# Seven half-size products for eight in the first layer of experts 1 to 3, with the tokens' combinations kept in DRAM

## The chip, the cores and the metric

The kernel runs on one core of a Trainium2 chip. The metric is device time in microseconds of that core. The core has a matrix engine (PE; its weight loads are listed apart as PEld), three engines for element-wise work (DVE, ACT, POOL), a queue that issues most DMA transfers (SP), an on-chip memory SBUF, eight PSUM banks of 2 KB per partition into which PE accumulates, and DRAM outside.

## The reference

Three stages run one after the other: a causal retention (linear attention with decay), a mixture of four experts in which every token passes through every expert, and a second mixture of eight experts in which each token goes to one. All inputs are float32. Only the second stage is changed. Cut to it:

```python
N, D, E, F = 2304, 512, 4, 1024
p = domain_probs / (domain_probs.sum(-1, keepdims=True) + 1e-09)
out = np.zeros((N, D))
for e in range(E):
    h = np.maximum(x @ w1[e], 0.0)          # the first layer: the part that is changed
    out += p[:, e:e + 1] * (h @ w2[e])
```

## The kernel before, in words

Every float32 operand of a matmul is split into two float16 numbers, a high and a low part, and a product is made of three float16 matmuls (high by high, high by low, low by high; `TERMS`). The split takes one ACT instruction (the high part) and one DVE instruction (the low part; `split`, lines 160 to 162).

The retention runs in 24 steps of 96 tokens (`at_load`, `at_split`, `at_a`, `at_b`). The output of a step is scaled by DVE (`xf`, line 269); ACT writes its high part and POOL its low part into the resident tile `xT` (lines 271 and 272), which holds all 2304 tokens. Steps 0 to 3 run ahead of everything; the other twenty are called between the matmuls of expert 0 (`at_hook`).

The second stage runs over four experts and, in each, over six blocks of 384 tokens; one expert with one block is called a pass here. A pass has eight units of the first layer (`l1`: 12 matmuls of 384 columns into one PSUM bank, then ACT writes relu's high part and DVE its low part into `ht`, lines 326 and 327) and three of the second (`l2`: 24 matmuls of 512 columns, then one ACT or DVE instruction into `acc`, lines 346 and 348). There are two banks (`ph`) for the first layer and two (`po`) for the second. The next expert's weights are loaded and split during the passes (`w_hook`: expert 1's in expert 0's last pass, the others' from the expert's third pass on). Through all passes of experts 1 to 3 the weights of the second mixture are loaded, split and stored back to DRAM (`s_hook`). In expert 3's passes, transposes and gate logits of the finished tokens (`g1`, `g2`, `g3`) stand between the other matmuls, in two PSUM banks of their own.

A scheduler lays the instructions out on each engine at build time, by the program's order and by what it takes to be ready. At run time each engine's queue is worked off in that order, and an instruction that waits on a semaphore holds up all that stand behind it on its engine. SP's queue of DMA issues works in the same way.

Of the kernel before, what the change touches and what calls it, by code (L numbers as in the profile page):

```python
# [9 lines left out]
F32 = mybir.dt.float32  # L10
# [11 lines left out]
C = 96  # L22
# [14 lines left out]
BIG = 65536.0  # L37
TERMS = ((0, 0), (0, 1), (1, 0))
# [63 lines left out]
def kernel(  # L102
# [48 lines left out]
    xT = x_p.tile([128, 2, KD, N], F16, name="xT")  # L151
# [4 lines left out]
    x1d = dram.tile([N, ROW], F32, name="x1d")  # L156
    w1d = dram.tile([E2 * 128, KD, 2, F], F16, name="w1d")
# [21 lines left out]
    raws, spl, pm, st = {}, {}, {}, {}  # L179

# [62 lines left out]
    def at_b(s):  # L243
# [52 lines left out]
    def w_split(e, i):  # L296
        r = rw.pop((e, i))
        if i < KD:
            w_parts(r, wt[e][0][:, i], None)
        else:  # L300
            j = 2 * (i - KD)
            w_parts(r, wt[e][1][:, j:j + 2], True)

# [4 lines left out]
    def l1(e, b, f, c0=0, c1=BT):  # L308
        w = wt[e][0]
        ph = ps.tile([128, BT], F32, tag="h", name="ph")  # L310
        t0 = b * BT
        n = 0
        for k in range(KD):
            for x, y in ((0, 0), (0, 1), (1, 0)):
                pe.matmul(  # L315
                    ph[:, c0:c1],
                    lhsT=w[:, k, x, f * 128:(f + 1) * 128],
                    rhs=xT[:, y, k, t0 + c0:t0 + c1],
# [4 lines left out]
        if c0 == 0:  # L323
            hts[f] = ht_p.tile([128, 2, BT], F16, tag="ht", name="ht")
        hi, lo, p = hts[f][:, 0, c0:c1], hts[f][:, 1, c0:c1], ph[:, c0:c1]
        pace["act"] = act.activation(out=hi, in_=p, func=ACTF.Relu)  # L326
        pace["dve"] = dve.scalar_tensor_tensor(out=lo, in0=p, scalar=0.0, in1=hi, op0=ALU.max, op1=ALU.subtract)  # L327

    def l2(e, b, i):
# [4 lines left out]
        for k in range(KF):  # L334
            for x, y in ((0, 0), (0, 1), (1, 0)):
                pe.matmul(  # L336
                    po,
                    lhsT=hts[k][:, x, i * 128:(i + 1) * 128],
# [15 lines left out]
    def s_load(i):  # L354
        e, j = divmod(i, 8)
        r = later["pool"].tile([128, 1024], F32, tag="sr", name="sr", bufs=2)
# [27 lines left out]

    def g1(t, pl):
        tp = later["ps"].tile([128, KD, 128], F32, tag="tp", name="tp")
# [6 lines left out]
    def g2(t):  # L393
        xs = x1h.pop(t)
        pg = later["ps"].tile([128, 2 * E2], F32, tag="pg", name="pg")
# [7 lines left out]
    def g3(b, pl):  # L403
# [13 lines left out]
        pr = later["ps"].tile([128, 2, TB * E2], F32, tag="pg", name="pr")  # L417
# [44 lines left out]
    def unpermute(pl, rr, tiles, n, name):  # L462

        pi = later["ps"].tile([128, n], F32, tag="pg", name="pi" + name)
# [152 lines left out]
    def m_open():  # L617
        x_ctx.close()
        p = ctx.enter_context(tc.tile_pool(name="m2", bufs=1, side="right"))
# [86 lines left out]
    def l1_part(c0, c1):  # L706
        for f in range(KF):
            l1(0, 0, f, c0 * C, c1 * C)
# [37 lines left out]
    wgr = const.tile([128, KD, 2 * E2], F32, name="wgr")  # L746
# [3 lines left out]
    ps_sum = const.tile([128, NT, 1], F32, name="ps_sum")  # L750
    dve.tensor_reduce(out=ps_sum, in_=p_sb, axis=AX.X, op=ALU.add)
    dve.tensor_scalar(out=ps_sum, in0=ps_sum, scalar1=1e-9, scalar2=None, op0=ALU.add)
    ps_inv = const.tile([128, NT, 1], F32, name="ps_inv")
# [10 lines left out]
    w_at = {}  # L764

    def at_hook():
# [191 lines left out]
```

## Time and profile before

| | |
|---|---|
| median of 3 runs | 1099.6 us (1098.09 to 1100.0) |
| the profiled execution, its own time | 1101.13 us |
| its span, first to last instruction | 1099.4 us |
| granted clock of PE, mean | 0.989 |
| busy: PE, DVE, ACT, POOL | 96%, 43%, 32%, 16% of the span |
| retention alone, before expert 0's second block | 0 to 92.46 us |
| expert 0's blocks 1 to 4, with retention between | 92.46 to 259.88 us |
| expert 0's block 5, then experts 1 and 2 | 259.88 to 680.30 us |
| expert 3 with the gate | 680.30 to 865.00 us |
| second mixture | 865.00 to 1099.4 us |

The span is the time between the first and the last instruction on the core; the profiled execution's own time is 1.7 us longer, and 1.5 us above the median. The busy share of an engine is an average over stages that differ; what counts for a change is the stage in which it works.

### The profile page before, as it was taken

What the parts mean: (1) busy time and instruction counts of PE and PEld (TensorE: products, weight loads), DVE (VectorE), ACT (ScalarE), POOL (GpSimd) and SP (SyncE); (2) the same over time, 40 slices, a digit from 0 to 9 for tenths busy, and PEclk for the clock granted to TensorE, in tenths of its full rate; (3) what the DMA queues carried; (4) which work ended last, traced back from release to release, by engine and by line L of the source; (5) the groups of instructions that cost most, each with busy time, mean ns of one, the idle gap of its engine ahead of it and who ended that gap; (6) DMA issues with size and microseconds to landing.
All of it is one profiled execution on the core that took longest, in us unless ns stands there. A gap on an engine that the chain in (4) does not pass through costs nothing.

```text
span 1099.4 us, 21060 instructions
## 1 busy us (share of the span) xinstructions
PE 1056.7 (96%) x9057; PEld 635.0 (58%) x9057; DVE 477.0 (43%) x935; ACT 352.1 (32%) x683; POOL 178.9 (16%) x160
## 2 busy tenths in 40 slices
PE   4789999999999999999999999999999999999996
PEld 3665555555555555555555555555555677777774
DVE  5966555654333455433344544544444511111111
ACT  5544444534322244321222432322221122222221
POOL 5655646620000000000000000000000021212121
PEclk9889999999999999999999999999999999999998
DMA  8552322102343566434446554344413262491692
GB/s 249 170 178 79 97 59 73 45 1 88 106 137 131 172 211 193 146 122 127 142 137 208 154 154 136 114 125 145 163 49 133 108 224 96 154 351 53 241 378 112
DMA packets 38514, 158.30 MB, mean 144 GB/s; under 512 B 4878, under 2 KB 5262, under 8 KB 36112
## 3 DMA queue, kind: packets, MB, share of 16 engines
q1 hardware_dynamic: 34896, 145.84, 40.4%
q0 software_dynamic: 3520, 11.06, 2.9%
q8 instruction: 73, 1.20, 0.5%
q14 instruction: 25, 0.20, 0.1%
HBM read 159.99 MB, written 43.55 MB: 185 GB/s over the span
## 4 chain that ended last, share of the span: by engine, by line
PE 68%; issue 11%; DMA 10%; POOL 5%; DVE 4%; ACT 1%; SPq 0%; POOLq 0%; DVEq 0%; ACTq 0%
PE po L336 32%; PE ph L315 31%; DMA out_dram<-y_s,sidxm 8%; DMA out_dram<-y_s,sidxe 2%; POOL vs L195 1%; PE xo L251 1%; PE sc L213 1%; POOL v L202 1%; POOL p L219 1%; DMA vkr<-in_vk_dram 1%; DVE w L162 1%; PE tp L388 1%; POOL sn L237 1%; DVE pf L217 1%; POOL xT L272 1%
## 5 line engine op out<-in xcount | busy, mean ns | idle before, releaser
L315 PE MATMUL ph<-xT,w 128*128 128x384 f16 (+1 forms) x2400 | 388.5, 321 | 9.5 <-DVE ht L327 5.4
L336 PE MATMUL po<-w,ht 128*128 128x512 f16 x1728 | 382.8, 380 | 0.1
L315 PEld LDWEIGHTS <-w 128*128 128x128 f16 x2400 | 231.5, 98 | 153.1 <-issue 11.2
L336 PEld LDWEIGHTS <-ht 128*128 128x128 f16 x1728 | 168.1, 98 | 197.9 <-issue 2.1
L326 ACT ACTIVATE ht<-ph 128x384 f16<-128x384 f32 (+1 forms) x200 | 95.2, 477 | 360.1 <-PE ph L315 359.9
L327 DVE SCALAR_TENSOR_TENSOR ht<-ph,ht 128x384 f16<-128x384 f32 (+1 forms) x200 | 107.2, 539 | 165.4 <-ACT ht L326 157.2
L348 DVE SCALAR_TENSOR_TENSOR acc<-po,p_sb,acc 128x512 f32<-128x512 f32 x54 | 40.5, 750 | 189.7 <-PE po L336 189.7
L664 PEld LDWEIGHTS <-lane 128*128 128x128 f16 x1920 | 109.0, 98 | 4.3 <-issue 0.2
L664 PE MATMUL p_h<-x_s,lane 128*128 128x128 f16 x1920 | 111.1, 219 | 0.0
L681 PE MATMUL p_y<-lane,h_s 128*128 128x512 f16 x480 | 107.2, 379 | 0.8 <-DVE h_s L674 0.8
L640 POOL DMA_INDIRECT x_g<-x1d,gidxe x3 | 3.2, 1060 | 593.0 <-PE ph L315 592.4
L674 DVE SCALAR_TENSOR_TENSOR h_s<-p_h,h_s 128x512 f16<-128x512 f32 x40 | 27.6, 691 | 158.3 <-ACT h_s L673 158.3
L162 DVE SCALAR_TENSOR_TENSOR s<-sr,s 128x512 f16<-128x512 f32 x128 | 82.7, 687 | 7.4 <-ACT s L161 7.4
L681 PEld LDWEIGHTS <-h_s 128*128 128x128 f16 x480 | 46.6, 98 | 52.6 <-DVE h_s L674 1.0
L161 ACT ACTIVATE s<-sr 128x512 f16<-128x512 f32 x128 | 73.0, 620 | 7.1 <-DMA w2d<-s 4.5
L673 ACT ACTIVATE h_s<-p_h 128x512 f16<-128x512 f32 x40 | 23.9, 597 | 78.5 <-PE p_h L664 78.5
L162 DVE SCALAR_TENSOR_TENSOR w<-wr,w 128x512 f16<-128x512 f32 x64 | 45.3, 745 | 0.5 <-ACT w L161 0.5
L683 ACT ACTIVATE y_s<-p_y,x_g 128x512 f32<-128x512 f32 x20 | 13.7, 687 | 92.5 <-PE p_y L681 78.8
L684 POOL DMA_INDIRECT out_dram<-y_s,sidxm x17 | 17.3, 1018 | 146.7 <-ACT y_s L683 138.1
L161 ACT ACTIVATE xs<-tp 128x512 f16<-128x512 f32 x18 | 10.7, 597 | 82.9 <-PE tp L388 82.9
L217 DVE TENSOR_TENSOR pf<-sc,ka 96x384 f32<-96x384 f32 x48 | 24.3, 546 | 28.9 <-PE sc L213 28.9
L195 POOL TENSOR_TENSOR vs<-vkr,ka 96x512 f32<-96x512 f32 x24 | 35.2, 1465 | 10.3 <-DMA ka<-in_ca_dram 7.3
(141 smaller groups left out, 655.7 us busy)
## 6 DMA issues: line engine op xcount, KB each, us to landing
lane<-w1d SPq DMA_DIRECT2D x20, 2048.0 KB, 9.3
lane<-w2d SPq DMA_DIRECT2D x20, 2048.0 KB, 9.2
wr<-in_w_dram SPq DMA_DIRECT2D x32, 512.0 KB, 6.3
sr<-in_w1s_dram SPq DMA_DIRECT2D x32, 512.0 KB, 4.3
w1d<-s SPq DMA_DIRECT2D x32, 512.0 KB, 5.2
sr<-in_w2s_dram SPq DMA_DIRECT2D x32, 512.0 KB, 4.3
w2d<-s SPq DMA_DIRECT2D x32, 512.0 KB, 5.3
qkr<-in_qk_dram SPq DMA_DIRECT2D x24, 384.0 KB, 4.3
```

The lines of the kernel that those rows point to most:

```text
L161: act.activation(out=hi, in_=raw, func=ACTF.Copy, scale=scale)
L162: dve.scalar_tensor_tensor(out=lo, in0=raw, scalar=scale, in1=hi, op0=ALU.mult, op1=ALU.subtract)
L195: pool.tensor_tensor(out=vs, in0=t[:, 0], in1=cst("vtab", H, 1)[:C].to_broadcast([C, H, D]), op=ALU.mult)
L217: dve.tensor_tensor(out=pf, in0=sc[r], in1=mask, op=ALU.mult)
L315: pe.matmul(ph[:, c0:c1], lhsT=w[:, k, x, f * 128:(f + 1) * 128], rhs=xT[:, y, k, t0 + c0:t0 + c1], start=(n == 0), stop=(n == 3 * KD - 1),)
L326: pace["act"] = act.activation(out=hi, in_=p, func=ACTF.Relu)
L327: pace["dve"] = dve.scalar_tensor_tensor(out=lo, in0=p, scalar=0.0, in1=hi, op0=ALU.max, op1=ALU.subtract)
L336: pe.matmul(po, lhsT=hts[k][:, x, i * 128:(i + 1) * 128], rhs=w[:, k, y], start=(n == 0), stop=(n == 3 * KF - 1),)
L348: dve.scalar_tensor_tensor(out=a, in0=po, scalar=p_sb[:, t, e:e + 1], in1=a, op0=ALU.mult, op1=ALU.add)
L664: pe.matmul(ph[:, j], lhsT=w[:, k, x, f * 128:(f + 1) * 128], rhs=xs[:, y, k], start=(n == 0), stop=(n == 3 * KD - 1),)
L674: dve.scalar_tensor_tensor(out=lo, in0=ph, scalar=0.0, in1=hi, op0=ALU.max, op1=ALU.subtract)
L681: pe.matmul(po, lhsT=h[:, a, k], rhs=w[:, k, b], start=(n == 0), stop=(n == 3 * KF - 1))
```

## The change

The four quarters of an expert's first weights (halves of the 512 inputs by halves of the 1024 hidden units) and the halves of a block's tokens and inputs are combined beforehand, so that a block's first layer takes seven products of half size in each dimension instead of eight (the Winograd form of Strassen's scheme). `PROD` names for each product the combination of weights (0 to 6) and of tokens (0 to 7). It applies to experts 1 to 3; expert 0 multiplies the plain halves as before.

- Tokens: step by step the retention writes its result into a tile `xc` of one block (two of them take turns) instead of `xT`. For every second pair of steps `at_mix` makes four combinations: four POOL instructions of 192 columns, one ACT instruction (high parts) and one DVE instruction (low parts) of 768. Each finished block is stored to DRAM (`xcd`). From expert 0's last pass on, `x_load` fetches the next block's combinations once a pass: 10,752 bytes per partition, 1344 KB in two transfers. There are 18 such loads.
- Weights: `w_mixed` makes 14 quarter splits of 512 columns (7 combinations for each of 2 row blocks) where `w_split` made 8, with 8 POOL additions or subtractions of 512 columns between them, in place, in the raw tiles. The second layer's weights are split as before (8 of 512 columns). This is done in 24 steps of one call each; in expert 0's last pass three are called per unit; the calls for experts 2 and 3 begin in the second pass of the expert before, one every third unit.
- First layer: `l1_mixed` has 14 units of 12 matmuls of 192 columns (seven products, each for two pairs of hidden blocks `j`). PSUM banks carry sums on from product to product: ACT copies bank x into bank y, bank q into SBUF (s5) and x into a new bank z; DVE adds s5 to x twice. `keep` makes relu's two parts eight times per pass, of 384 columns each, as before. Per pass this adds six ACT copies and four DVE additions.
- PSUM: the new banks y and q (two each) take the four banks that were left, so the gate of expert 3 shares the two `po` banks until `m_open`. The raw tiles of both mixtures' weights share one pool of four buffers.

The core of the diff (left out: renamed tiles, unchanged parts of the loops):

```diff
+PROD = {1: (0, 0), 2: (1, 1), 4: (2, 7), 5: (3, 4), 6: (4, 5), 7: (5, 6), 3: (6, 3)}
...
+    def at_mix(s):
+        xa, xb = xfs.pop(s - 2), xfs.pop(s)
+        b, r = divmod(s, 4)
+        m = at_1.tile([128, 4, 2, C], F32, name="xm", bufs=1)
+        pool.tensor_tensor(out=m[:, 0], in0=xb[:, 0], in1=xa[:, 0], op=ALU.subtract)
...
+        act.activation(out=hi, in_=m, func=ACTF.Copy)
+        dve.tensor_tensor(out=lo, in0=m, in1=hi, op=ALU.subtract)
+        if r == 3:
+            sp.dma_start(out=xcd[b * 128:(b + 1) * 128], in_=xcs[b])
+    def x_load(b):
+        t = x_p.tile([128, 2, 8, 2, HB], F16, tag="xc", name="xc")
+        src = xcd[b * 128:(b + 1) * 128]
+        sp.dma_start(out=t[:, :, 0:2], in_=src[:, :, 0:2])
+        sp.dma_start(out=t[:, :, 3:], in_=src[:, :, 3:])
...
+        def rows(k, more):
+            steps.append(lambda: put(k, 3, 2))
+            steps.append(lambda: (mix(k, 3, 1, 3, ALU.add), put(k, 0, 0)))
+            steps.append(lambda: (mix(k, 1, 0, 1, ALU.subtract), put(k, 2, 1)))
+            steps.append(lambda: (mix(k, 0, 3, 0, ALU.subtract), put(k, 3, 3)))
+            steps.append(lambda: (mix(k, 2, 2, 0, ALU.subtract), put(k, 1, 5)))
+            steps.append(lambda: (put(k, 0, 4), more[0]()))
+            steps.append(lambda: (put(k, 2, 6), more[1]()))
...
+            for i in range(2):
+                f = (2 * j + i) * 128
+                n = 0
+                for k in range(2):
+                    for u, v in TERMS:
+                        pe.matmul(
+                            bank[:, i], lhsT=w[:, k, u, f:f + 128], rhs=x[:, v, d, k],
+                            start=(first and i == 0 and n == 0), stop=(n == 5), skip_group_check=True,
+                        )
...
+        def m7(j):
+            x_, s5 = t[j]["x"], t[j]["s"]
+            mm(x_, 7, j)
+            z = t[j]["z"] = bank("y", later["mix"])
+            cp = act.activation(out=z, in_=x_, func=ACTF.Copy)
+            ad = dve.tensor_tensor(out=s5, in0=x_, in1=s5, op=ALU.add)
...
+            keep(s5, out_to(1, j, 1))
...
+        for m in (m1, m5, m6, m2_, m7, m3, m4):
+            for j in range(2):
+                units.append(lambda m=m, j=j: m(j))
...
+    def g_bank(tag, shape, name=None):
+        if "ps" in later:
+            return later["ps"].tile(shape, F32, tag=tag, name=name or tag)
+        return ps.tile(shape, F32, tag="o", name=name or tag)
...
+                if u == 0 and e + (b == NB - 1) and (e, b) != (E1 - 1, NB - 1):
+                    x_load((b + 1) % NB)
```

POOL's queue at the end of retention step 7, the last of token block 1, before. `sn` is a state, `p`, `v` and `vs` belong to later steps, `xT` is step 7's low part:

```order
L237 TENSOR_TENSOR sn<-sn,ka 128x256 [waits DVE_49]
L219 TENSOR_TENSOR p_1435<-pf,p_1435 96x384 [waits Activation_49]
L202 TENSOR_TENSOR v_1559<-vs,v_1559 96x512 [waits Activation_49]
L195 TENSOR_TENSOR vs<-vkr,ka 96x512 [waits DMAHW6_49,Pool_49]
L272 TENSOR_TENSOR xT<-xf,xT 128x4x96 [waits Activation_49]
```
The same place now; `xm` are combinations of the step's tokens, `xc` is step 7's low part (the 128x4x96 row):

```order
L241 TENSOR_TENSOR sn<-sn,ka 128x256 [waits DVE_49]
L223 TENSOR_TENSOR p_1455<-pf,p_1455 96x384 [waits Activation_49]
L206 TENSOR_TENSOR v_1579<-vs,v_1579 96x512 [waits Activation_49]
L199 TENSOR_TENSOR vs<-vkr,ka 96x512 [waits DMAHW5_49,Pool_49]
L291 TENSOR_TENSOR xm<-xf 128x192 [waits DVE_49]
L292 TENSOR_TENSOR xm<-xf 128x192
L283 TENSOR_TENSOR xc<-xf,xc 128x4x96 [waits Activation_49]
```
Two combinations now stand between `vs` and the low part that the next pass's first matmuls read.

DVE's queue in expert 0's last pass before: `ht` is the low part of a first-layer unit, `w_1` are expert 1's weights:

```order
L162 SCALAR_TENSOR_TENSOR w_1_4337<-wr,w_1_4337 128x512 [waits Activation_49]
L327 SCALAR_TENSOR_TENSOR ht<-ph,ht 128x384 [waits Activation_49]
L162 SCALAR_TENSOR_TENSOR w_1_4337<-wr,w_1_4337 128x512 [waits Activation_49] x2
L327 SCALAR_TENSOR_TENSOR ht<-ph,ht 128x384 [waits Activation_49]
L162 SCALAR_TENSOR_TENSOR w_1_4337<-wr,w_1_4337 128x512 [waits Activation_49] x2
L327 SCALAR_TENSOR_TENSOR ht<-ph,ht 128x384 [waits Activation_49]
L162 SCALAR_TENSOR_TENSOR w_1_4337<-wr,w_1_4337 128x512 [waits Activation_49] x2
L327 SCALAR_TENSOR_TENSOR ht<-ph,ht 128x384 [waits Activation_49]
```
The same place now (4419 and 4421 are the two tiles of expert 1's first weights):

```order
L389 SCALAR_TENSOR_TENSOR ht<-ph,ht 128x384 [waits Activation_49]
L165 SCALAR_TENSOR_TENSOR w_1_4419<-wr,w_1_4419 128x512 [waits DMAHW3_49,DVE_49,Activation_49]
L389 SCALAR_TENSOR_TENSOR ht<-ph,ht 128x384 [waits Activation_49]
L165 SCALAR_TENSOR_TENSOR w_1_4419<-wr,w_1_4419 128x512 [waits Activation_49] x3
L389 SCALAR_TENSOR_TENSOR ht<-ph,ht 128x384 [waits Activation_49]
L165 SCALAR_TENSOR_TENSOR w_1_4421<-wr,w_1_4421 128x512 [waits Activation_49] x3
L389 SCALAR_TENSOR_TENSOR ht<-ph,ht 128x384 [waits Activation_49]
L165 SCALAR_TENSOR_TENSOR w_1_4419<-wr,w_1_4419 128x512 [waits Activation_49] x3
L389 SCALAR_TENSOR_TENSOR ht<-ph,ht 128x384 [waits Activation_49]
```
Between two `ht` rows of this stretch stood two weight splits; now there are three.

ACT's queue in a pass of expert 1 before (`s` are second-mixture weights, `w_2` expert 2's):

```order
L326 ACTIVATE ht<-ph 128x384 [waits PE_49] x2
L161 ACTIVATE s_5377<-sr 128x512 [waits DMAHW1_49,DMAHW0_49,DVE_49]
L161 ACTIVATE s_5377<-sr 128x512
L326 ACTIVATE ht<-ph 128x384 [waits PE_49]
L161 ACTIVATE w_2_5086<-wr 128x512 x2
L326 ACTIVATE ht<-ph 128x384 [waits PE_49] x2
L161 ACTIVATE s_5439<-sr 128x512 [waits DMAHW3_49,DMAHW2_49,DVE_49]
L161 ACTIVATE s_5439<-sr 128x512
L326 ACTIVATE ht<-ph 128x384 [waits PE_49]
L161 ACTIVATE w_2_5086<-wr 128x512 x2
```
And now, in the second pass of expert 1: `py<-ph` and the two `s<-pq` rows are copies between banks and to s5, the `ht` rows are relu's high parts:

```order
L454 ACTIVATE py<-ph 128x384 [waits PE_49]
L454 ACTIVATE py<-ph 128x384 [waits DVE_49,PE_49]
L460 ACTIVATE s_5053<-pq 128x384 [waits PE_49]
L460 ACTIVATE s_5068<-pq 128x384 [waits PE_49]
L388 ACTIVATE ht<-py 128x2x192 [waits PE_49,Activation_49] x2
L164 ACTIVATE w_2_5033<-wr 128x512 [waits DMAHW2_49]
L474 ACTIVATE py<-ph 128x384 [waits DVE_49,PE_49] x2
L388 ACTIVATE ht<-s_5053 128x2x192 [waits DVE_49]
L164 ACTIVATE s_5157<-sr 128x512 [waits DMAHW4_49,DMAHW3_49]
L164 ACTIVATE s_5157<-sr 128x512
L388 ACTIVATE ht<-s_5068 128x2x192 [waits DVE_49]
L388 ACTIVATE ht<-pq 128x2x192 [waits PE_49]
```
The copies stand ahead of the stage splits, and the last `ht` rows of the pass behind them.

## Rows read from the trace of the kernel before

**Rows 1.** windows: length in us, each engine's busy us (instructions), clock, DMA share, GB/s.

```profile
92.46:259.88 167.42, 160.85 (x2041) 95.14 (x2040) 93.11 (x141) 72.42 (x140) 79.39 (x68) 1.00 0.19 56
259.88:291.02 31.14, 31.14 (x169) 16.45 (x168) 14.47 (x24) 14.39 (x27) 0.00 (x0) 1.00 0.46 153
291.02:680.30 389.28, 389.28 (x2113) 206.66 (x2112) 166.33 (x271) 119.85 (x236) 0.00 (x0) 1.00 0.48 149
```

**Rows 2.** waits of PE: who waited for whom, us in total, times, longest.

```profile
PE xo L251 <- POOL p L219: 5.9, 4, 3.0
PE ph L315 <- DVE ht L327: 5.4, 5, 1.8
```

**Rows 3.** timeline of PE, full-width passes: start, us, engine, line, instruction, count.

```profile
259.88 15.76 PE L315 MATMUL ph<-xT,w 128*128 128x384 f16 x96
275.48 15.70 PE L336 MATMUL po<-w,ht 128*128 128x512 f16 x72
291.02 15.76 PE L315 MATMUL ph<-xT,w 128*128 128x384 f16 x96
```

**Rows 4.** timeline of PE, 192-column matmuls of the first pass.

```profile
45.96 2.14 PE L315 MATMUL ph<-xT,w 128*128 128x192 f16 x24 [0.18 <-DVE ht L327]
48.03 0.36 PE L251 MATMUL xo<-p,v 96*64 96x96 f16 x7
...
59.10 4.12 PE L315 MATMUL ph<-xT,w 128*128 128x192 f16 x48
63.15 0.38 PE L213 MATMUL sc<-x 64*96 64x96 f16 x7
```

**Rows 5.** timeline of PE, 128-column matmuls of the second layer.

```profile
891.26 5.52 PE L664 MATMUL p_h<-x_s,lane 128*128 128x128 f16 x96
896.62 0.61 PE L652 MATMUL p_t<-kb,x_g 128*128 128x128 f32 x4
```

**Rows 6.** groups by line: instructions, busy us, mean ns, idle before.

```profile
L315 PEld LDWEIGHTS <-w 128*128 128x128 f16 x2400 | 231.5, 98 | 153.1 <-issue 11.2 <-DVE w L162 0.4
...
L327 DVE SCALAR_TENSOR_TENSOR ht<-ph,ht 128x384 f16<-128x384 f32 (+1 forms) x200 | 107.2, 539 | 165.4 <-ACT ht L326 157.2
...
L326 ACT ACTIVATE ht<-ph 128x384 f16<-128x384 f32 (+1 forms) x200 | 95.2, 477 | 360.1 <-PE ph L315 359.9
...
L348 DVE SCALAR_TENSOR_TENSOR acc<-po,p_sb,acc 128x512 f32<-128x512 f32 x54 | 40.5, 750 | 189.7 <-PE po L336 189.7
```

**Rows 7.** timeline, expert 1's weight splits in expert 0's last pass.

```profile
272.17 1.14 ACT L161 ACTIVATE w<-wr 128x512 f16<-128x512 f32 x2
272.31 0.56 DVE L327 SCALAR_TENSOR_TENSOR ht<-ph,ht 128x384 f16<-128x384 f32 x1
272.83 1.29 DVE L162 SCALAR_TENSOR_TENSOR w<-wr,w 128x512 f16<-128x512 f32 x2
```

**Rows 8.** timeline, DVE beside POOL in the attention passes.

```profile
58.17 0.62 DVE L162 SCALAR_TENSOR_TENSOR k<-vkr,k 96x512 f16<-96x512 f32 x1
...
146.18 1.16 POOL L202 TENSOR_TENSOR v<-vs,v 96x512 f16<-96x512 f32 x1 [0.17 <-ACT v L201]
146.21 2.54 DVE L162 SCALAR_TENSOR_TENSOR k<-vkr,k 96x512 f16<-96x512 f32 x1
...
147.29 0.91 POOL L272 TENSOR_TENSOR xT<-xf,xT 128x384 f16<-128x384 f32 x1
...
149.27 2.11 PE L315 MATMUL ph<-xT,w 128*128 128x384 f16 x12 [1.76 <-DVE ht L327]
```

**Rows 9.** timeline, the start of block 1's pass, and an undisturbed POOL row.

```profile
92.32 0.91 POOL L272 TENSOR_TENSOR xT<-xf,xT 128x384 f16<-128x384 f32 x1
...
93.28 5.85 PE L315 MATMUL ph<-xT,w 128*128 128x384 f16 x35 [0.49 <-POOL xT L272]
...
125.26 1.04 POOL L195 TENSOR_TENSOR vs<-vkr,ka 96x512 f32<-96x512 f32 x1
```

**Rows 10.** DMA issues: name, engine, count, KB each, median us to landing.

```profile
lane<-w1d SPq DMA_DIRECT2D x20, 2048.0 KB, 9.3
```

More of the change, by code (lines that the diff above doesn't have):

```diff
@@ L302, in w_split, with w_mixed, quarter, put @@
             w_parts(r, wt[e][1][:, j:j + 2], True)
+    def w_mixed(e):
+        steps = []
+        def quarter(k, i):
+            r = rw[e, k + 2 * (i // 2)]
+            return r[:, 512 * (i % 2):512 * (i % 2) + 512]
+        def put(k, i, c):
+            t = wt[e][0][:, c, k] if c < 4 else wt[e][2][:, c - 4, k]
+            split(quarter(k, i), t[:, 0], t[:, 1], S_W)
+        def mix(k, to, x, y, op):
+            pool.tensor_tensor(out=quarter(k, to), in0=quarter(k, x), in1=quarter(k, y), op=op)
+        def rows(k, more):
[6 more added lines that the diff above has]
+            steps.append(lambda: (put(k, 2, 6), more[1]()))
+        def part(i, h):
+            r = rw[e, i][:, 512 * h:512 * h + 512]
+            t = wt[e][1][:, 2 * (i - KD) + h]
+            split(r, t[:, 0], t[:, 1], S_W)
+        def ld(i):
+            return lambda: w_load(e, i)
+        steps.append(lambda: (w_tiles(e), w_load(e, 0), w_load(e, 2)))
+        steps.append(lambda: None)
+        rows(0, (ld(1), ld(3)))
+        rows(1, (ld(4), ld(5)))
+        for i in range(KD, 8):
+            steps.append(lambda i=i: part(i, 0))
+            steps.append(lambda i=i: (part(i, 1), w_load(e, i + 2) if i + 2 < 8 else None))
+        return steps
@@ L305, with keep, l1_first @@
     hts = {}
     pace = {}
[L308 to L311, printed above, removed]
+    def keep(src, dst):
+        pace["act"] = act.activation(out=dst[0], in_=src, func=ACTF.Relu)
+        pace["dve"] = dve.scalar_tensor_tensor(
+            out=dst[1], in0=src, scalar=0.0, in1=dst[0], op0=ALU.max, op1=ALU.subtract
+        )
+    def l1_first(b, f, h0=0, h1=2):
+        w = wt[0][0].rearrange("p a b c f -> p (a b c f)").rearrange("p (k x f) -> p k x f", k=KD, x=2)
+        x = xcs[b]
+        ph = ps.tile([128, 2, HB], F32, tag="h", name="ph")
@@ L322, in l1 @@
                 n += 1
[L323 to L327, printed above, removed]
+        if f % 2 == 0 and h0 == 0:
+            hts[f // 2] = ht_p.tile([128, 2, 2, BT], F16, tag="ht", name="ht")
+        c = slice(h0 * HB, h1 * HB)
@@ L333, in l2 @@
         n = 0
-        for k in range(KF):
+        for k in (0, 1, 4, 5, 2, 3, 6, 7):
             for x, y in ((0, 0), (0, 1), (1, 0)):
@@ L355, in s_load @@
         e, j = divmod(i, 8)
-        r = later["pool"].tile([128, 1024], F32, tag="sr", name="sr", bufs=2)
+        r = raw_p.tile([128, 1024], F32, tag="wr", name="sr")
         if j < KD:
@@ L394, in g2 @@
         xs = x1h.pop(t)
-        pg = later["ps"].tile([128, 2 * E2], F32, tag="pg", name="pg")
+        pg = g_bank("pg", [128, 2 * E2])
         n = 0
@@ L462, in unpermute @@
     def unpermute(pl, rr, tiles, n, name):
-        pi = later["ps"].tile([128, n], F32, tag="pg", name="pi" + name)
+        pi = g_bank("pg", [128, n], "pi" + name)
         for t in range(tiles):
@@ L618, in m_open @@
         x_ctx.close()
+        mix_ctx.close()
+        later["ps"] = ctx.enter_context(tc.tile_pool(name="later_ps", bufs=1, space=PSUM))
         p = ctx.enter_context(tc.tile_pool(name="m2", bufs=1, side="right"))
@@ L745 @@
     w_first(7)
-    wgr = const.tile([128, KD, 2 * E2], F32, name="wgr")
+    wgr = at_1.tile([128, KD, 2 * E2], F32, name="wgr")
     sp.dma_start(out=wgr, in_=wg)
@@ L838 @@
                 if e == 0 and nxt[0] >= NSTEP and b == NB - 1:
-                    w_hook(1)
-                if e and e + 1 < E1 and b >= 2 and u in (1, 4, 7):
+                    for _ in range(3):
+                        w_hook(1)
+                if e and e + 1 < E1 and b >= 1 and u % 3 == 1:
                     w_hook(e + 1)
-                if e and u in (0, 3, 6, 9):
+                if e and u in (0, 4, 8, 12):
                     s_hook()
```

151 lines of the change are left out of this document (112 added, 39 removed).

## The prediction

> **What bounds the kernel now.** I read the busy shares by stretch first, then what PE waits for, then PE's own timeline, and last the rows of the engines that the change loads. From 259.88 us to the end of expert 2 PE is busy for the whole of both stretches (31.14 of 31.14 us, 389.28 of 389.28) at a granted clock of 1.00, its 2.4 GHz level, with POOL at nothing [rows 1]. So in the passes of the second mixture layer by layer nothing but the matmul stream sets the time, and a matmul saved there is time saved as long as no wait takes its place. In the retention stretch PE has 167.42 − 160.85 = 6.6 us idle [rows 1]; over the whole span its longest waits are for POOL's low part `p` (5.9) and DVE's relu part (5.4) [rows 2]. There POOL and DVE already decide when PE goes on, and the change gives them more to do.
>
> **What the products save.** A pass is 15.60 us of first layer (275.48 − 259.88, 96 matmuls, 162.5 ns each) and 15.54 of second [rows 3]. It gets 7 products x 4 hidden blocks x 2 row blocks x 3 terms = 168 matmuls of 192 columns. Such matmuls ran in the first pass: 24 took 48.03 − 45.96 = 2.07 us and 48 took 63.15 − 59.10 = 4.05 [rows 4]; the second 24 thus cost 1.98, 82.5 ns each, and the rest (0.09 us) is the change of shape at the end of a run. 168 x 82.5 ns = 13.86 us, 1.74 saved per pass, 18 passes: −31.3 us. Bounds: half of a 384-column matmul (81.25 ns) gives 13.65 and −35; 4.05 / 48 = 84.4 ns gives 14.18 and −25.6. Two matmuls of 384 columns that fill the new banks once add 0.3.
>
> Each of the 168 has its own weight load, 72 more per pass. In the second mixture 96 matmuls of only 128 columns start every 55.8 ns (896.62 − 891.26 = 5.36) [rows 5], so loads keep up with a faster stream than this. The Trainium skill, TensorE: Matmul & The Clock Gate, section Back-to-back issue gap, says the opposite: in a real stream load and matmul together set the spacing, about 81 ns at 128 columns. This case's 55.8 ns disagrees with that; by the rule the gain would be mostly gone.
>
> **The passes of expert 0 with retention in them (+8).** Ten steps here each add four POOL instructions of 192 columns. POOL took 0.91 us for 384 columns [rows 9], so about 0.46 each. They go in front of, or between, POOL's other work. At the start of block 1's pass PE waited 0.49 us for the low part of the block's last step [rows 9]; now two combinations stand before it, and before block 2's three. So these four waits grow by 1.0, 1.4, 1.0, 1.0: +4.4. DVE's low half of a combination (768 columns, two SBUF inputs) is about 0.9 us, four of them fall beside the relu parts on which PE waited 5.4 us already [rows 2]: another 3.6. Bounds: zero, if POOL's idle time takes it all (it is busy 79 of 167 us [rows 1]), and 4 x 8 x 0.46 = 15 if none does. I take 8, the sum of the two, since the waits are already in the trace.
>
> **Before 92.46 us (+2).** The combinations of steps 2 and 3 are laid in here too, though the program calls for them later. Eight POOL instructions, 3.7 us, are the upper bound, zero the lower; half is my choice.
>
> **Expert 0's last pass (+7).** This is where the change is hardest on DVE. Before, two splits (1.29 us) and one relu part (0.56) fitted a unit of 1.95 us (15.60 / 8) [rows 3, 7]. Now three splits stand between relu parts, and 8 POOL instructions feed them. Unit 7 needs the bank that unit 5's relu part frees; ahead of that in DVE's queue stand 13 splits (8.4 us) and, with its own, five relu parts (2.8). The first of all ends 3.2 us into the pass (unit 0 at 1.95, ACT 0.48 [rows 6], DVE 0.56 and some 0.2 for the signals between). 3.2 + 8.4 + 2.8 = 14.4 against 7 x 1.95 = 13.65 when PE wants it: 0.8 late. That holds if POOL doesn't hinder DVE. But a DVE split of 512 columns that takes 0.62 us alone took 2.54 when it began with POOL at work: POOL ran `v` and then `xT` and DVE got no turn until they were over, and PE lost 1.76 us to it [rows 8]. POOL's undisturbed 512-column float32 instruction took 1.04 [rows 9]; 8 x 1.04 = 8.3 more makes it 9.1 late. If the relu parts, which read PSUM, run beside POOL, up to 2.8 come back: I take 7, near the row that shows the conflict, between 0 (ACT and DVE a little quicker than counted) and 9.
>
> The Trainium skill, SBUF — State Buffer, section SBUF: two separate sides, states it as a rule: POOL and a DVE instruction with two SBUF inputs hold a common port in turn, each for its whole length. The trace agrees (2.54 against 0.62). By the rule alone the term is the upper bound.
>
> **The steady passes (+4).** Per pass ACT gets six copies (about 0.48 each [rows 6]) and DVE four additions; both were idle more than half the time [rows 1]. Along a pass, in units of 12 x 82.5 ns = 0.99 us: y is copied by 1.7 and 2.8 us and PE adds onto it from 5.9; DVE's first sums are in q at 5.8 and 6.8, wanted at 9.9 and 10.9; the copy into z ends at 9.7 and 10.7 (one weight split ahead of it), wanted at 11.9 and 12.9. Slack everywhere is 2 us or more. What follows is tighter: the relu parts of the last four sums stand behind two stage splits on ACT and DVE, and the second layer's first tile reads z's low part some 1.7 us after it begins (13.9 + 8 x 0.216). By my count that part ends at about 16.0 where 15.6 is wanted. So 0 to one DVE split (0.65 [rows 7]) per pass, 0 to 12 us; I take 4, since only the ten passes with weight work have the full queue.
>
> **Expert 3 (+2).** The gate shares two banks with `po`, so the third tile of a pass waits for the second one's DVE sum (0.75 [rows 6]), with 12 short gate matmuls and 8 of 192 columns (0.66) to fill: 0.3 per pass, six passes; 0 to 4.5.
>
> **Transfers (0).** 18 loads of 1344 KB; 2048 KB landed in 9.3 us [rows 10], and a load is issued a pass (29 us) ahead.
>
> **Sum.** −31.3 + 0.3 + 8 + 2 + 7 + 4 + 2 = −8.0. The profiled execution took 1101.1, so 1093.1; it stood 1.5 above the median, so 1091.6, rounded 1092. About 0.2% (2.2 us) is what a measurement of this kernel can tell from no change.
>
> **The rivals.**
> - *Everything is covered.* Idle time on POOL and DVE takes the new work, the last pass of expert 0 loses 2, the retention passes 3: −31.3 + 0.3 + 5 = −26, 1074. For it: DVE is busy 93 and POOL 79 of the 167 us with retention [rows 1]. Against it: the waits on POOL and DVE are already on PE's path [rows 2].
> - *Each pass ends in a wait for ACT's queue.* ACT holds two stage splits before the last four relu parts; a stage load that lands late stops the queue, relu comes late, and PE stands at each second layer. From (31.3 − 0.3 − 8 − 2 − 7 − 2) / 18 = 0.67 us per pass the change is slower; at 1.5 us, 27 in place of 4 makes 1115. For it: it recurs 18 times. Against it: DMA is at 0.48 and the same splits cost PE nothing before [rows 1].
> - *The token load is late.* It stands on SP behind weight loads that wait for raw buffers which DVE and POOL free. Beyond 8.0 / 18 = 0.44 us per pass the change is slower: at 1 us each, 18 more, 1110. For it: the queue works in order. Against it: nearly a pass of time to land.
> - *Weight loads set the pace.* A weight load takes 98 ns [rows 6]. If a narrow matmul could start only when a load of its own had run, 168 of them would be 16.5 us, 0.9 more than before instead of 1.74 less, and the time 1138. For it: loads nearly double. Against it: 55.8 ns at 128 columns [rows 5]. This is the mechanism of the rule on spacing named above.
>
> **Chances.** The forecast 0.50, with a range of its own from 1082 to 1101; everything covered 0.22; the wait for ACT 0.17; the late load 0.05; weight loads 0.03; small mishaps of both signs 0.03. Faster by over 0.2%: 0.42 of the forecast, 0.22, and 0.01 of the rest, 0.65. Slower: 0.14 of the ACT rival, 0.04, 0.03 and 0.01, 0.22. No change: 0.13, mostly the forecast's upper end. The range 1072 to 1110 leaves out some 0.06 below and 0.13 above.
>
> **What would show it.** Right: passes of experts 1 and 2 of 29.4 to 30.1 us, 168 matmuls of 192 columns in about 13.9 with no wait between products; in expert 0's last pass the first layer longer by some 7 us, PE waiting for `ht`, DVE's splits far over 0.65 beside POOL; waits for `xc`'s low part of 1.5 to 2.5 at four block starts. Wrong: a first layer of 14.5 or more without waits (spacing), a wait for `ht` at each second layer (ACT's queue), a wait for `xc` by DMA (the load), or the last pass of expert 0 at its old length.

## The result, and the profile after

The changed kernel took 1111.09 us (median of 4 runs, 1110.12 to 1112.86) against 1099.8 us (4 runs): a ratio of 1.0106 with an interval of 1.0087 to 1.0124. It is slower by some 11 us, where 8 us less was forecast; the range ended at 1110. The profiled execution has a span of 1109.3 us, 9.9 more than before.

The stretches of the changed kernel, from the same boundaries as in [rows 1] (length, busy us and instructions of PE, PEld, DVE, ACT and POOL, clock, DMA share, GB/s):

```profile
0.00:93.20 93.20, 66.47 (x1009) 49.07 (x1010) 69.62 (x113) 52.03 (x103) 61.53 (x59) 0.95 0.63 200
93.20:285.74 192.54, 169.83 (x2041) 97.88 (x2041) 100.63 (x151) 79.36 (x149) 101.22 (x105) 0.95 0.26 87
285.74:323.95 38.21, 31.78 (x170) 16.42 (x169) 25.49 (x33) 19.01 (x35) 12.54 (x8) 1.00 0.60 215
323.95:693.43 369.48, 367.67 (x3051) 264.65 (x3050) 203.55 (x331) 157.92 (x324) 23.29 (x16) 1.00 0.60 205
```

The retention stretch grew from 167.42 to 192.54 us, expert 0's last pass from 31.14 to 38.21; experts 1 and 2 shrank from 389.28 to 369.48. PE's idle time in the retention stretch is 22.7 us instead of 6.6, and its granted clock 0.95 instead of 1.00. What PE waits for (us, times, longest), as in [rows 2]:

```profile
PE ph L401 <- POOL xc L283: 15.0, 5, 4.5
PE ph L401 <- DVE ht L389: 13.8, 11, 2.7
PE ph L401 <- ACT xc L282: 6.0, 5, 2.1
PE po L504 <- DVE ht L389: 1.5, 2, 0.8
```

The first and third have grown. Before, the same waits were:

```profile
PE ph L315 <- POOL xT L272: 2.9, 5, 1.0
PE ph L315 <- ACT xT L271: 0.8, 1, 0.8
```

Four of the five waits of each row stand at the starts of the passes of blocks 1 to 4, where the first matmuls read the high (L282) and the low part (L283) of the block's last retention step. PE at these four starts; the first answers to [rows 9]:

```profile
93.20 0.32 PE L401 MATMUL ph<-xc,w 128*128 128x384 f16 x1 [1.15 <-ACT xc L282]
96.86 7.53 PE L401 MATMUL ph<-xc,w 128*128 128x384 f16 x35 [3.34 <-POOL xc L283]
...
141.22 0.32 PE L401 MATMUL ph<-xc,w 128*128 128x384 f16 x1 [1.16 <-ACT xc L282]
146.04 8.76 PE L401 MATMUL ph<-xc,w 128*128 128x384 f16 x35 [4.50 <-POOL xc L283]
...
193.10 0.32 PE L401 MATMUL ph<-xc,w 128*128 128x384 f16 x1 [2.06 <-ACT xc L282]
196.77 7.31 PE L401 MATMUL ph<-xc,w 128*128 128x384 f16 x35 [3.34 <-POOL xc L283]
...
238.88 0.32 PE L401 MATMUL ph<-xc,w 128*128 128x384 f16 x1 [0.87 <-ACT xc L282]
242.55 8.30 PE L401 MATMUL ph<-xc,w 128*128 128x384 f16 x35 [3.35 <-POOL xc L283]
```

And at the start of block 2's pass before:

```profile
135.97 5.85 PE L315 MATMUL ph<-xT,w 128*128 128x384 f16 x35 [1.00 <-POOL xT L272]
```

Two things are to be read here. The waits: before, 1.00 us at block 2's start and 0.49 at each of the others; now 1.16 + 4.50 at block 2's and 4.22 to 5.40 at the others. And the 35 matmuls behind them, the same instructions that took 5.85 us at every start before, now take 7.31 to 8.76. The windows behind the second wait say why (the clock is the third number from the end):

```profile
146.00:148.00 2.00, 1.96 (x7) 0.95 (x7) 0.56 (x1) 1.42 (x2) 0.53 (x1) 0.50 0.00 0
148.00:150.00 2.00, 2.00 (x8) 0.97 (x7) 0.40 (x1) 0.25 (x1) 0.00 (x0) 0.50 0.47 197
...
152.00:154.00 2.00, 2.00 (x14) 1.19 (x13) 0.56 (x1) 0.49 (x1) 0.00 (x0) 1.00 0.47 197
```

After the idle time PE runs at 0.50, its 1.2 GHz level: 7 or 8 matmuls in 2 us instead of 14. The Trainium skill, TensorE: Matmul & The Clock Gate, section HAM oscillation — how this bites in real kernels, warns of matmuls that come back slow after such gaps; the trace agrees.

Why the low part is late is seen on the queues of the other engines ahead of block 2's pass (POOL, ACT, DVE in turn; `xm` are the combinations):

```profile
134.04 0.59 POOL L294 TENSOR_TENSOR xm<-xf,xm 128x192 f32<-128x192 f32 x1
...
134.66 0.84 ACT L297 ACTIVATE xc<-xm 128x768 f16<-128x768 f32 x1 [5.45 <-POOL xm L294]
...
135.54 0.96 DVE L298 TENSOR_TENSOR xc<-xm,xc 128x768 f16<-128x768 f32 x1 [5.75 <-ACT xc L297]
136.41 1.01 DVE L221 TENSOR_TENSOR pf<-sc,ka 96x384 f32<-96x384 f32 x2
```

The same `pf` before, when it waited for PE's scores alone:

```profile
127.91 1.02 DVE L217 TENSOR_TENSOR pf<-sc,ka 96x384 f32<-96x384 f32 x2 [3.39 <-PE sc L213]
```

DVE stood idle for 5.75 us in front of L298, the low part of the combinations, which waits for ACT's high part, which waits for POOL's last combination. Behind it in DVE's queue stands `pf` of the next retention step, whose scores PE had finished by 133.2. It began 4.01 us after PE's first score matmul (132.40), before 0.77 us (127.14); at the four starts it is 2.8 to 4.0 us later than before. So the whole step starts late, its POOL work with it, and then three combinations (0.58 us each) stand in front of the low part that PE wants. Over the program DVE was idle for 48.6 us in front of 11 of these low parts, ACT 47.6 us in front of 11 high parts.

The steady passes went as forecast: in an undisturbed one the products take 13.86 us (353.67 to 367.53) and the second layer 15.54 (338.13 to 353.67), against 15.60 and 15.54 in [rows 3].

```profile
338.13 15.70 PE L504 MATMUL po<-w,ht 128*128 128x512 f16 x72
353.67 2.14 PE L430 MATMUL ph<-xc,w 128*128 128x192 f16 x24
...
365.55 2.14 PE L430 MATMUL py<-xc,w 128*128 128x192 f16 x24
367.53 1.89 PE L504 MATMUL po<-w,ht 128*128 128x512 f16 x8
```

### The profile page after: what moved, and what is told of

Read it like the earlier page. It is cut to its first block, busy times and chain, and to the rows that moved or that the text cites. A ratio compares the mean times of both kernels' runs of the same rounds, so it can differ in the third digit from the quotient of the medians.

```text
span 1109.3 us, 24208 instructions
## 1 busy us (share of the span) xinstructions
PE 1038.6 (94%) x10355; PEld 716.2 (65%) x10355; DVE 541.5 (49%) x1037; ACT 417.2 (38%) x821; POOL 243.6 (22%) x232
## 4 chain that ended last, share of the span: by engine, by line
PE 57%; DMA 12%; issue 11%; DVE 9%; POOL 8%; ACT 2%; SPq 0%; POOLq 0%; ACTq 0%; DVEq 0%
PE po L504 27%; PE ph L430 9%; DMA out_dram<-y_s,sidxm 8%; PE ph L401 6%; PE pq L430 5%; PE py L430 5%; DVE w L165 2%; DMA out_dram<-y_s,sidxe 2%; POOL vs L199 2%; DVE ht L389 2%; POOL v L206 1%; DVE s L165 1%; POOL sn L241 1%; POOL p L223 1%; DVE pf L221 1%
## 5 line engine op out<-in xcount | busy, mean ns | idle before, releaser
L430 PEld LDWEIGHTS <-w 128*128 128x128 f16 x3024 | 249.2, 98 | 4.5
L401 PE MATMUL ph<-xc,w 128*128 128x384 f16 (+1 forms) x672 | 112.1, 326 | 35.4 <-POOL xc L283 15.0
L430 PE MATMUL ph<-xc,w 128*128 128x192 f16 x1296 | 119.1, 246 | 0.0
L401 PEld LDWEIGHTS <-w 128*128 128x128 f16 x672 | 67.0, 105 | 76.5 <-issue 48.1
L165 DVE SCALAR_TENSOR_TENSOR s<-sr,s 128x512 f16<-128x512 f32 x128 | 90.4, 747 | 49.2 <-ACT s L164 46.1
L353 POOL TENSOR_TENSOR wr<-wr 128x512 f32<-128x512 f32 x24 | 35.8, 1493 | 263.8 <-DVE w L165 262.8
L430 PE MATMUL pq<-xc,w 128*128 128x192 f16 x864 | 79.8, 246 | 0.0
L430 PE MATMUL py<-xc,w 128*128 128x192 f16 x864 | 77.2, 246 | 0.0
L165 DVE SCALAR_TENSOR_TENSOR w<-wr,w 128x512 f16<-128x512 f32 x82 | 68.0, 858 | 1.0 <-ACT w L164 0.7
L388 ACT ACTIVATE ht<-py 128x384 f16<-128x384 f32 x72 | 35.3, 490 | 48.6 <-PE py L430 48.6
L464 DVE TENSOR_TENSOR pq<-ph,s 128x384 f32<-128x384 f32 x36 | 20.3, 565 | 66.6 <-PE ph L430 66.0
```

The source lines that it names most:

```text
L165: dve.scalar_tensor_tensor(out=lo, in0=raw, scalar=scale, in1=hi, op0=ALU.mult, op1=ALU.subtract)
L353: pool.tensor_tensor(out=quarter(k, to), in0=quarter(k, x), in1=quarter(k, y), op=op)
L388: pace["act"] = act.activation(out=dst[0], in_=src, func=ACTF.Relu)
L401: pe.matmul(ph[:, h0:h1], lhsT=w[:, k, u, f * 128:(f + 1) * 128], rhs=x[:, v, k // 2 + 2 * h0:k // 2 + 2 * h1 - 1:2, k % 2], start=(n == 0 ...
L430: pe.matmul(bank[:, i], lhsT=w[:, k, u, f:f + 128], rhs=x[:, v, d, k], start=(first and i == 0 and n == 0), stop=(n == 5), skip_group_chec ...
```

## The experiments

My theory (queue): the combination parts on ACT and DVE wait for POOL at the head of their queues and make the next retention step late; POOL's combinations then stand ahead of the low part; PE's longer waits bring the clock down. Rival (work): the added work costs its time wherever it stands. For expert 0's last pass: POOL's sums slow DVE (port) against too many splits (count).

### Combinations in the next pass

```diff
-        if s % 4 > 1:
-            at_mix(s)
+        if s % 4 < 2:
+            with tc.issue_after(los[s - s % 4 - 1].ins), tc.issue_after(pace["act"].ins), tc.issue_after(pace["dve"].ins):
+                at_mix(s - 2)
```

The edit also gives the step outputs `xf` eight buffers instead of six, since they are kept longer. That is not what helped: in the changed kernel DVE's `xf` never waited for a buffer (its only waits, 0.9 us in all, are for PE).

> The four combinations of a step pair, their high part on ACT and their low part on DVE are issued in the next pass, behind that pass's relu parts, instead of ahead of the next retention step; the work is the same. Queue theory (ACT's and DVE's combination parts wait for POOL at the head of their queues, and the next step's chain behind them is 3.3 us late; then PE waits over 3 us and its clock falls): the stretch from 93.20 to 285.74 (192.5 us) falls to 168 to 173, PE's waits for xc at the four block starts to about 0.5 each, the clock there stays at 1.00, and the time is 1086 to 1092. Work theory (the added POOL, ACT and DVE work costs its time wherever it stands): the stretch stays at 185 or more, the time at 1103 or more.

Measured: 1095.45 us (ratio 0.9966, 0.9952 to 0.9980), the stretch 173.71 us instead of 192.54, the waits at the four starts back to 0.49 and 1.00, the clock at 0.99. The queue theory holds for 18.8 of the 25.1 us, and the work theory, which wanted 185 us or more, falls. Why 173.7 and not 170, and 1095 and not 1092, shows in DVE and PE in block 2's pass:

```profile
149.95 2.80 DVE L298 TENSOR_TENSOR xc<-xm,xc 128x768 f16<-128x768 f32 x1
...
155.27 3.06 PE L401 MATMUL ph<-xc,w 128*128 128x384 f16 x12 [4.02 <-DVE ht L389]
```

The low part of 0.96 us now took 2.80 beside POOL's `v` and `xc`, ahead of a relu part, for which PE waited 4.02 us where it had waited 1.76 [rows 8]; the 12 matmuls behind it then took 3.06 us instead of 2.11. And the stretch before it ended at 95.68 instead of 93.20.

### Only ACT's and DVE's parts in the next pass

```diff
         if s % 4 > 1:
             at_mix(s)
+        if s % 4 < 2:
+            with tc.issue_after(pace["act"].ins), tc.issue_after(pace["dve"].ins):
+                at_parts(s - 2)
```

`at_parts` is the second half of `at_mix`, the instructions of ACT and DVE. The edit also gives the combinations (`xm`) three buffers instead of one, since they are kept longer.

> Only the high part (ACT) and the low part (DVE) of the combinations are issued in the next pass; POOL's combinations stay where they were, ahead of the block's last low part. Queue theory: what remains at a block start is two or three POOL combinations of 0.58 us ahead of the low part, so waits of 1.6 to 2.2 us at four starts, no half clock, a stretch of 172 to 178 us and 1091 to 1097. If POOL's combinations are the cause: waits stay above 3 us, the clock falls as before, the stretch stays at 185 or more, 1104 or more.

Measured: 1104.88 us (1.0049, 1.0034 to 1.0064); stretch 183.11 us, in a profiled execution of 1108.93. Neither theory met its figures: three of the four waits at the starts (1.01, 2.64, 2.32 and 2.22 us) and the stretch lie between the two, and the time is in the range of the theory that blamed POOL's combinations. PE at the starts of blocks 2 to 4, with two waits for relu parts ahead of and between them:

```profile
114.02 3.79 PE L406 MATMUL ph<-xc,w 128*128 128x384 f16 x12 [2.00 <-DVE ht L394]
...
146.91 5.85 PE L406 MATMUL ph<-xc,w 128*128 128x384 f16 x35 [2.64 <-POOL xc L283]
...
161.91 3.79 PE L406 MATMUL ph<-xc,w 128*128 128x384 f16 x12 [3.47 <-DVE ht L394]
...
194.87 7.53 PE L406 MATMUL ph<-xc,w 128*128 128x384 f16 x35 [2.32 <-POOL xc L283]
...
240.90 5.85 PE L406 MATMUL ph<-xc,w 128*128 128x384 f16 x35 [2.22 <-POOL xc L283]
```

The waits at the four starts are 0.52, 1.64, 1.83 and 1.73 us above those of before, 5.7 together. In POOL's order nine combinations of 0.58 us, 5.2 us, still stand ahead of the four low parts (three at block 2, two at each of the others). So of the 17.3 us that the four starts had lost (4.3 each), 5 to 6 are POOL's combinations and, by subtraction, the other 12 or so the two queues. The stretch is 15.7 us longer than before: those 5.7; 4.8 of longer waits for relu parts, which the parts, now in the first layer, delay (3.47 us in block 2 instead of 1.76); and 5.0 of half clock, since the clock fell three times, after 2.00, 3.47 and 2.32 us, and each time the matmuls behind took 1.68 us more (3.79 for 2.11, 7.53 for 5.85). The prologue ended at 98.51 us instead of 93.20; the cause of that stays open.

### Expert 1's weight sums left out

```diff
-            pool.tensor_tensor(out=quarter(k, to), in0=quarter(k, x), in1=quarter(k, y), op=op)
+            if e > 1:
+                pool.tensor_tensor(out=quarter(k, to), in0=quarter(k, x), in1=quarter(k, y), op=op)
```

> Expert 1's eight POOL sums of weight quarters are left out (its products then use uncombined quarters); the 14 quarter splits, the copies and everything else stay. Port theory (POOL's two-input instructions hold up DVE's splits): expert 0's last first layer goes from 22.9 us (285.74 to 308.62) to 16 to 17.5, and the time is 1104 to 1106. Count theory (three DVE splits between two relu parts are too many by themselves): it stays at 21 us or more, 1109 or more.

Measured: the first layer of expert 0's last pass took 16.3 us (285.25 to 301.56), the pass 31.64 instead of 38.21. DVE in it, and in the changed kernel:

```profile
290.39 1.90 DVE L165 SCALAR_TENSOR_TENSOR w<-wr,w 128x512 f16<-128x512 f32 x3
```

```profile
290.88 4.04 DVE L165 SCALAR_TENSOR_TENSOR w<-wr,w 128x512 f16<-128x512 f32 x3
```

The same three splits take 1.90 us without POOL and 4.04 beside it. The port theory holds, the count theory falls. The edit takes away a second thing, the waits of splits for POOL's results; but DVE was idle for 3.1 us of this first layer in the changed kernel and 2.8 here, while its busy time fell from 19.8 to 13.5 us, so the difference is in the length of its instructions and not in waits. The whole time, 1124.01 us, missed its figure: from expert 3's last second layer on it took 270.4 us instead of 250.8, with 2874 matmuls instead of 2626. The values of expert 1 are others without the sums, so the tokens probably take other routes in the second mixture. Only the stretches ahead of it can be compared.

### A first combination of repairs

```diff
-                    for _ in range(3):
+                    for _ in range(1 if u < n1 else 5):
                         w_hook(1)
...
-                    if gate:
+                    if gate and (u >= n1 or u % 2 == 0):
                         gate.pop(0)()
```

This is the first edit with expert 1's weight steps spread over the whole pass and the gate's pieces at every second first-layer unit.

> The first edit above, with expert 1's weight steps called once per first-layer unit and five times per second-layer tile of expert 0's last pass (one is left for expert 1's second unit), and the gate's pieces called only at every second unit of expert 3's first layers. Queue and port theories: the retention stretch 168 to 173 us, expert 0's last pass 31 to 34 instead of 38.2, expert 3's passes 31.8 to 32.3 instead of 32.8: 1076 to 1084. Work theory: 1098 or more.

Measured: 1087.74 us (0.9892, 0.9875 to 0.9908). Expert 0's last pass 31.96 us, expert 3 from its first to its last second layer 163.6 instead of 165.1 us; the retention stretch 173.7 as in the first experiment. That, expert 3's passes (32.7 us on average where 31.8 to 32.3 were expected) and a prologue of 95.03 us instead of 93.20 kept it above 1084.

### Combinations in the first two units of the next pass

```diff
+                if e == 0 and 0 < b < NB - 1 and u < 2:
+                    mix_after(4 * b + 2 + u)
```

The other blocks' combinations are taken out of `at_hook`; block 0's go behind that block's last low part as well, and `xf` has eight buffers, as in the first experiment.

> As the first experiment, but the two combination steps of a block stand in the first two units of the next pass, where POOL and DVE are idle, instead of its third and sixth unit, where the next retention steps keep POOL busy. Port theory (in the first experiment a 768-column low part took 2.80 us beside POOL and held up the relu parts): the retention stretch falls from 173.7 to 168 to 171 us, PE's waits for relu parts in it back to about 6, and the time is 1090 to 1093. Rival (the same work delays relu parts by as much in the first units): 173 or more and 1095 or more.

Measured: 1103.07 us (1.0021, 1.0012 to 1.0030), stretch 178.01 us: a miss; the prologue ended at 96.57. The order within the units was right, but the second set of combinations had no buffer (POOL, ACT, DVE):

```profile
146.36 0.59 POOL L291 TENSOR_TENSOR xm<-xf 128x192 f32<-128x192 f32 x1 [2.01 <-DVE xc L298]
...
148.75 0.85 ACT L297 ACTIVATE xc<-xm 128x768 f16<-128x768 f32 x1 [2.24 <-POOL xm L294]
...
149.63 0.96 DVE L298 TENSOR_TENSOR xc<-xm,xc 128x768 f16<-128x768 f32 x1 [2.53 <-ACT xc L297]
```

DVE's low part (0.96 us, so nothing slows it here) waited 2.53 us at the head of its queue, ahead of the third relu part and the next step. It is the same chain of waits as in the changed kernel, only in another place. What I had put down to the port alone was in good part again a queue; the port is there too (in the same place a split of 512 columns took 2.54 us).

### The gate in the first layer only

```diff
-                    if gate:
+                    if gate and (b == NB - 1 and u >= n1 or u < n1 and (u % 2 == 0 or u == n1 - 1)):
```

> Only the gate of expert 3 is changed against the changed kernel: its pieces are called at every second first-layer unit of the next pass, none beside the second layer (except in the last pass). If the gate's chain (transpose, split, logits) is exposed because units are half as long, and the two shared banks hold up the second layer's third tile: a pass of expert 3 falls from 32.8 to 31.6 to 31.9 us, the time to 1105 to 1107. If the extra 1.1 us per pass is the gate's matmuls themselves: 32.5 or more, 1110 or more.

Measured: 1119.34 us (1.0163, 1.0138 to 1.0188): a miss of the wrong sign. Expert 3 from its first to its last second layer took 170.2 us instead of 165.1: the last gate piece of a pass and the early routing came later, and PE waited 3.8 us for `oh` and 4.4 us at once for the routing's `err`, after which 29 matmuls of the second layer took 8.52 us instead of 6.42.

### The second combination of repairs

The two edits above with the weight steps spread (one per first-layer unit, four per tile of the second, four left for expert 1's first pass).

> The two edits of this batch together with expert 1's weight steps spread (one per first-layer unit, four per second-layer tile of expert 0's last pass, the last four in expert 1's first pass): retention stretch 168 to 171, expert 0's last pass 31.2 to 32, a pass of expert 3 of 31.6 to 31.9: 1077 to 1083. If the first units do not hide the combinations: 1084 or more.

Measured: 1101.34 us (1.0002, 0.9993 to 1.0011). Expert 0's last pass took 31.96 us as wanted, the retention stretch 178.2 and the routing wait 4.4, as in the two kernels above.

### Two buffers for the combinations

```diff
-        m = at_1.tile([128, 4, 2, C], F32, name="xm", bufs=1)
+        m = at_1.tile([128, 4, 2, C], F32, name="xm", bufs=2)
```

> The fifth kernel (combinations in the first two units of the next pass) with two buffers for the combinations instead of one. With one, POOL's second set waited 2.01 us for DVE's low part of the first, and ACT (2.24) and DVE (2.53) waited for that set ahead of a relu part. Queue theory: with two buffers nobody waits at the head of a queue there; the retention stretch falls from 178.0 to 168 to 171 us, the waits for relu parts from 21.6 to 13 to 15 us (7 to 8 of them in expert 0's last pass), the time to 1089 to 1094. If the combinations' work itself is what costs: 175 or more, 1100 or more.

Measured: 1092.45 us (0.9931, 0.9914 to 0.9949), stretch 170.33 us. The row that answers to the one above:

```profile
144.48 0.96 DVE L298 TENSOR_TENSOR xc<-xm,xc 128x768 f16<-128x768 f32 x1 [0.89 <-ACT xc L297]
```

DVE's wait fell from 2.53 to 0.89, and with it the stretch by 7.7 us and the prologue by 2.0, by a buffer alone, with the same instructions. That shows without any change of work that an instruction waiting at the head of a queue is what costs. PE's waits for relu parts fell from 21.6 to 15.8 us, a little above the expected 13 to 15.

### The best version

The kernel above with expert 1's weight steps and the gate spread:

```diff
-                    for _ in range(3):
+                    for _ in range(1 if u < n1 else 4):
                         w_hook(1)
+                if e == 1 and b == 0 and u in (1, 3, 5, 7):
+                    w_hook(1)
...
-                    if gate:
+                    if gate and (u >= n1 or u % 2 == 0):
```

> The kernel before this one in the batch, with expert 1's weight steps spread as in the second best version and the gate spaced as in the first (pieces beside the second layer as before, every second unit in the first). Queue and port theories: stretch 168 to 171, expert 0's last pass 31.5 to 32.5, passes of expert 3 of 32.2 to 32.6: 1080 to 1085. Otherwise 1088 or more.

Measured: 1083.1 us (5 runs, 1081.18 to 1083.63; ratio 0.9848, 0.9833 to 0.9863), faster than both kernels, with the same arithmetic as the changed one. Its stretches:

```profile
93.88:263.19 169.31, 160.88 (x2042) 95.11 (x2040) 101.65 (x151) 80.60 (x150) 104.45 (x109) 1.00 0.29 98
263.19:295.15 31.96, 31.30 (x170) 16.43 (x169) 22.59 (x29) 16.75 (x32) 11.86 (x8) 1.00 0.49 171
295.15:664.76 369.61, 367.77 (x3051) 264.61 (x3050) 206.95 (x336) 159.41 (x328) 23.33 (x16) 1.00 0.62 213
664.76:827.73 162.97, 161.48 (x1468) 115.55 (x1467) 88.20 (x278) 57.39 (x124) 0.00 (x0) 1.00 0.41 145
```

POOL is busy for as long in the first stretch (104 us against 101) and DVE too; the 23 us less than in the changed kernel are order and buffers, and 1.9 us of the 25.1 are left. In expert 0's last pass POOL still slows nine splits to 10.04 us, but beside the second layer, where only ACT's accumulation is waited for (0.66 us).

### Block 0's combinations out of the prologue

```diff
-        if s in (4, 5):
-            mix_after(s - 2)
...
+                if e == 0 and b == 1 and u < 2:
+                    mix_after(2 + u)
+                if e == 0 and b == 1 and u in (2, 3):
+                    mix_after(4 + u)
```

The lines left out make each set wait for the newest low part instead of its own block's.

> The same, with block 0's two combination steps moved out of the prologue, where POOL lays them ahead of the next state, into the first units of the second pass (block 1's into its third and fourth unit). Prologue back from 95 to 96.6 us to 92.5 to 93.5, block 1's pass 0 to 3 us longer than in the kernel before this one: 1077 to 1084. If the four combination steps hold up that pass's relu parts: 1086 or more.

Measured: 1085.82 us (0.9874, 0.9851 to 0.9896): not better. The prologue ended at 90.99 us instead of 93.88, but block 1's pass, now with four combination steps, took 48.2 us instead of 43.2: PE waited 4.67 us for a relu part instead of 1.39, and the 12 matmuls behind it took 4.00 us instead of 2.11.

## Why the prediction was wrong, step by step

Differences of the two profiled executions, by the same boundaries; the terms add to −8.0 forecast and to +9.9 measured.

| step | forecast | measured |
|---|---|---|
| seven products for eight, with the fill matmuls | −31.0 | −31.0 where nothing waits (13.86 us per first layer) |
| steady passes | +4 | +2.5 |
| before 92.46 | +2 | +0.7 |
| retention passes | +8 | +25.1 |
| expert 0's last pass | +7 | +7.1 |
| expert 3's gate | +2 | +5.8 |
| from expert 3's last second layer on | 0 | −0.3 |

**What was right.** The products: 168 matmuls in 13.86 us to the digit, so weight loads do not set the pace. The steady passes wait only twice for relu parts at their second layer, 1.5 us together, where the prediction had allowed 4 us in ten passes, and the token loads never hold up PE. Expert 0's last pass lost its time for the reason given, POOL beside DVE's splits as in the port row [rows 8]: the third experiment removes POOL's sums and the pass is back at 31.64. That the figure of 7 fits to a tenth is luck, since it was taken from between 0 and 9.

**The step that failed: the retention passes.** The prediction priced the new instructions there by their durations: "DVE's low half of a combination (768 columns, two SBUF inputs) is about 0.9 us", and POOL's combinations at 4.4 in all, with an upper bound of 15. The duration was right (0.95 us). But the instruction waits for ACT and that for POOL, so it holds its queue for up to 5.75 us. At the four starts, where 1.5 to 2.5 us of wait for the low part had been named as the sign of being right, 3.34 to 4.50 came. The prediction had read POOL's order at this place, and not DVE's, where the low part stands directly ahead of `pf`. The measured 25.1 come apart so, over four starts: the waits for the high part grew by 5.2 (1.15 + 1.16 + 2.06 + 0.87), those for the low part by 12.1 (14.53 against 2.47), and the half clock after them cost 8.5 (31.90 us for the four runs of 35 matmuls against 23.40); the rest, −0.7, is spread. Of the 17.3 of waits 5 to 6 are POOL's combinations (nine of 0.58 us in POOL's order, 5.7 us left in the second experiment), more than the 4.4 counted, since a combination of 192 columns took 0.58 us and not 0.46; the other 12 or so are, by subtraction, the two queues. The prediction's second failure is in the bound: 15 us counted instructions alone, no wait in front of one, and no clock.

The rival "each pass ends in a wait for ACT's queue" named this kind of wait, an engine held at the head of its queue by another's result, but in the steady passes, where it did not come. None of the rivals put it in the retention passes, though the prediction says of them that POOL and DVE already decided there when PE went on.

**Expert 3 (+5.8, bound 4.5).** Its passes went from 33.41 to 32.78 us, 1.1 short of the 1.74. The trace shows gaps too short to be listed as waits, around gate pieces that now come after 8 narrow matmuls:

```profile
712.40 0.33 PE L430 MATMUL pq<-xc,w 128*128 128x192 f16 x2
712.76 0.21 PE L572 MATMUL pg<-wg_sb,xs 128*128 128x16 f16 x2
712.83 0.82 PE L430 MATMUL pq<-xc,w 128*128 128x192 f16 x8
```

Two matmuls of 82.5 ns end 0.2 us before the logits begin. Wider spacing gave 0.55 us back in three of five passes of the best version (32.21 to 32.23); the other two took 33.1 and 33.2, two of the changed kernel 33.2 and 33.6; moving the pieces out of the second layer too made the routing late. How the remaining half microsecond divides between the shared banks and these gaps stays open; a gate with banks of its own was not tried, since all eight are in use.

## What to carry to other kernels

Price a new instruction by where it stands in its queue: what it waits for, and what stands behind it; its duration is the smaller part when it depends on another engine. Where a stage already shows waits on the path, put helper work for later behind the chain that is wanted next, with as many buffers as steps that follow one another, and away from a partner on the shared port. And where a wait on the matrix engine grows to some microseconds, price the clock too.

## What the runs showed of the hardware that was not expected

- The half clock cost half as much again as the waits did: 8.5 us on top of 17.3. In the changed kernel it came after each wait of 3.34 to 4.50 us, but elsewhere also after 2.00 us (second experiment) and 2.18 (two buffers), and not after 2.96 (combinations in the first two units). The same unit of expert 0's last pass, after the same wait, in the changed kernel and in that with two buffers:

```profile
306.68 2.11 PE L401 MATMUL ph<-xc,w 128*128 128x384 f16 x12 [2.69 <-DVE ht L389]
```

```profile
285.85 3.79 PE L401 MATMUL ph<-xc,w 128*128 128x384 f16 x12 [2.69 <-DVE ht L389]
```

  The granted clock was 1.00 in the first and 0.54 in the second. So the length of a wait alone does not tell it.
- POOL is slowed by DVE as DVE is by POOL: its 512-column sums of weights took 1.49 us on average where an undisturbed 512-column instruction took 1.04 [rows 9]. The Trainium skill, SBUF — State Buffer, section SBUF: two separate sides, lets whichever began first finish while the other waits. The trace agrees that both can lose: DVE's split took 2.54 us instead of 0.62 [rows 8].
